# Normalizing the first block of rows ahead of the second's last statistics, in column parts, with a bias transposed by DMA and two loads merged

## The chip, the cores and the metric

The kernel runs on one core of a Trainium2 chip. The metric is the device time of one execution in microseconds (us), taken over several executions; lower is better. A difference counts as faster or slower from 2% (4.3 us) on. The span is the time from the first to the last instruction of a trace; the time of an execution is some 2 us longer. A few executions are in a slower state, in which the granted clock of TensorE is lower; unless said otherwise the compared runs are in the fast state.

## The reference, cut to what matters

```python
# B, S, D = 1, 2048, 640; H = 32 heads of 20; F = 1536; bf16
x  = A_x
xn = _layernorm(x, axis=-1)
return x + _A_ref(xn, A_wqkv, A_wo) + _B_ref(xn, B_w1, B_b1, B_w2, B_b2)
# _A_ref: q, k, v = xn @ wqkv; each position attends to 8 positions, 2 apart, then @ wo
# _B_ref: gelu(xn @ w1 + b1) @ w2 + b2
```

## The kernel before

The rows are handled in four chunks of 512, each of four blocks of 128. Every piece of work is a task with an engine, a rank, a duration, and an earliest time (`after`, used where a load has to land). A list scheduler at build time puts the tasks of TensorE (PE), VectorE (DVE), ScalarE (ACT) and the queue of SyncE (SP) in a fixed order. The engines then run in that order, whatever the real times are.

In chunk 0 each block goes through statistics, square root (ACT), reciprocal and normalization (DVE), five transposes (PE), and a copy out of PSUM (ACT). Then come its q, k and v projections, `gps`:

```python
# plan, chunk 0
land = (3.2, 3.2, 6.6, 6.6)[bl] if n == 0 else 11.4 + 1.9 * n
pl.add(f"st{n}{bl}", VE, 1.17, -40 if n else -99, [], f("st", n, bl), after=land)
pl.add(f"rs{n}{bl}", SE, 0.35, -99, [f"st{n}{bl}"], f("sqrt", n, bl, bl + 1), table="sqrt")
pl.add(f"rc{n}{bl}", VE, 0.17, -99, [f"rs{n}{bl}"], f("rstd", n, bl, bl + 1))
...
def do_tp(n, bl):                                  # five transposes into one PSUM tile
    xn = tiles["xn", n, bl]
    tp = psA.tile([P, 2 * CH], BF16, tag="acc", name="tp")
    for t in range(KT):
        nc.tensor.transpose(tp[:, t * P : (t + 1) * P], xn[:, t * P : (t + 1) * P], ident[:])
...
# loads, in the order in which SP issues them
nc.sync.dma_start(x_sb[:, 0, :], x_nb[:, 0, :])
for s in range(3):                                 # wq, wk, wv
    nc.sync.dma_start(wqkv[s][:], wqkv_v[:, :, s * D : (s + 1) * D])
    if s == 0:
        nc.sync.dma_start(x_sb[:, 2:BPC, :], x_nb[:, 2:BPC, :])
nc.sync.dma_start(b1_rt[0:FT, :], B_b1.rearrange("(t p) -> t p", p=P))
for n in range(1, NCH):                            # x of chunks 1, 2, 3
    ...
nc.sync.dma_start(w1_sb[:], B_w1.rearrange("(t p) n -> p t n", p=P))
...
def bias1():                                       # between k and v of block 0, on PE
    nc.tensor.transpose(b1_tp[:, 0:FT], b1_rt[0:FT, :], ident[0:FT, 0:FT])
    nc.vector.tensor_copy(b1T[:], b1_tp[:, 0:FT])
```

After chunk 0's projections come the first layer of the MLP (`hps`), the other chunks' projections (`pps`), the logits (`L`, which need the DVE's products `prod`), and the output (`lo`, `hi`).

## Time and profile before

| before | value |
|---|---|
| time, median of the first three executions | 215.12 us |
| time of the profiled execution | 215.21 us |
| PE busy | 206.1 us, 97% of a span of 212.9 us |
| first `gps` (first real dense matmul) | 7.70 us |
| first k projection; landing of wk | 9.93; 9.6 us |
| first `hps` | 25.32 us |
| last output piece on DVE | starts at 210.14 us |

The page's busy shares and chain, TensorE's list of waits and the head are shown with the prediction. One stretch is not shown there. It is the timeline of DVE around 10 to 14 us. The columns are start, duration, engine, line, operation, output and inputs, count, and in brackets the idle time before it and what ended that.

```profile
9.83 0.17 DVE L398 RECIPROCAL rstd<-std 128x1 f32<-128x1 f32 x1
9.91 0.27 DVE L363 TENSOR_REDUCE head_of<-ident 128x32 bf16<-128x128 bf16 x1
10.10 0.45 DVE L415 TENSOR_SCALAR xn<-x_sb,mv,rstd 128x640 bf16<-128x640 bf16 x1
12.47 0.17 DVE L370 CAST b1T<-b_tp 128x12 f32<-128x12 bf16 x1 [1.93 <-PE b_tp L369]
13.70 0.49 DVE L388 BATCH_NORM_STATS2 stats<-x_sb 128x6 f32<-128x320 bf16 x1 [1.05 <-DMA x_sb<-in_A_x_dram]
```

The `xn` at 10.10 is the last block of chunk 0. It is done 3 us before DVE turns to the statistics of chunk 1, for which it waits until x lands at 13.70.

The timeline of PE in the same kernel has the first k projection, b1's transpose, and the first `hps`:

```profile
9.93 1.28 PE L489 MATMUL gps<-xnT,wk_sb 128*128 128x128 bf16 x20
...
12.26 0.18 PE L369 MATMUL b_tp<-ident,b_rt 12*128 12x12 bf16 x1
...
25.32 1.03 PE L637 MATMUL hps<-xnT,w_sb 128*128 128x512 bf16 x3
```

### The profile page before, as it was taken

The numbers are of one execution on the slowest core, as the hardware profiler recorded it, in microseconds if no ns is written. First come the engines' busy times: TensorE is split into PE (matmuls) and PEld (weight loads), VectorE is DVE, ScalarE is ACT, GpSimd is POOL, SyncE is SP. The second block draws the span as 40 slices with busy tenths as digits, with TensorE's granted clock in tenths as the row PEclk, the third lists the DMA queues.
The fourth block names the chain that finished last, engine by engine and source line by source line (L and its number), as shares of the span: only waits on it lengthen the run. The fifth ranks groups of instructions, "written<-read, shape, count | busy, mean of one in ns | idle before, by whom it ended". The sixth has DMA issues, their size and how long they took to land.

```text
span 212.9 us, 3943 instructions
## 1 busy us (share of the span) xinstructions
PE 206.1 (97%) x1665; PEld 121.2 (57%) x1690; DVE 174.2 (82%) x176; ACT 106.8 (50%) x190; POOL 19.5 (9%) x36
## 2 busy tenths in 40 slices
PE   7899999999999999999999999999999999999994
PEld 7799844654544556556555555554555455555552
DVE  2849999459999999999999999999499789982001
ACT  3567899689565733635428273420297321351210
POOL 2000000000011015101001010110101011101220
PEclk9999999999999999999999999999999999999999
DMA  6999417973939579977002180211021822202223
GB/s 211 364 363 381 78 31 198 386 67 41 228 115 140 76 261 211 197 115 190 0 3 31 17 210 4 31 7 27 2 31 14 216 32 31 26 8 32 34 31 62
DMA packets 23433, 23.95 MB, mean 112 GB/s; under 512 B 9080, under 2 KB 20600, under 8 KB 23416
## 3 DMA queue, kind: packets, MB, share of 16 engines
q1 hardware_dynamic: 17832, 16.49, 28.0%
q0 software_dynamic: 4144, 4.92, 17.3%
q10 hardware_dynamic: 1440, 2.29, 3.7%
q8 instruction: 13, 0.21, 0.4%
q14 instruction: 4, 0.03, 0.0%
HBM read 10.00 MB, written 7.54 MB: 82 GB/s over the span
## 4 chain that ended last, share of the span: by engine, by line
PE 95%; DMA 1%; DVE 1%; issue 1%; ACT 0%
PE lo L668 26%; PE hps L637 24%; PE pps L472 23%; PE gps L489 8%; PE hi L670 8%; PE L L541 4%; DMA x_sb<-in_A_x_dram 1%; PE tp L429 0%; DVE stats L388 0%; DVE stats L389 0%; ACT xnT L433 0%; DVE xn L415 0%; DVE mv L390 0%; DVE osb L698 0%; PE b_tp L369 0%
## 5 line engine op out<-in xcount | busy, mean ns | idle before, releaser
L637 PE MATMUL hps<-xnT,w_sb 128*128 128x512 bf16 x236 | 53.9, 379 | 0.3 <-issue 0.2
L668 PE MATMUL lo<-w_sb,hT 128*128 128x512 bf16 x186 | 52.6, 379 | 0.0
L615 DVE TENSOR_TENSOR pv<-vT,ax 128x2560 bf16<-128x2560 bf16 x32 | 45.9, 1484 | 4.9 <-PE L L541 2.9
L522 DVE TENSOR_TENSOR prod<-qT,kT 128x2560 bf16<-128x2560 bf16 x32 | 45.5, 1484 | 0.0
L670 PE MATMUL hi<-w_sb,hT 128*128 128x128 bf16 x192 | 40.3, 219 | 0.3
L648 ACT ACTIVATE hT<-hps,b1T 128x512 bf16<-128x512 f32 x48 | 31.4, 687 | 17.0 <-PE hps L637 13.7
L637 PEld LDWEIGHTS <-w_sb 128*128 128x128 bf16 x240 | 22.8, 98 | 26.8 <-issue 0.4
L675 ACT CAST osb<-lo 128x512 bf16<-128x512 f32 x15 | 8.8, 585 | 50.9 <-PE hi L670 22.9
L624 DVE TENSOR_TENSOR pv<-pv 128x5120 bf16<-128x5120 bf16 x12 | 33.9, 2822 | 0.3
L668 PEld LDWEIGHTS <-hT 128*128 128x128 bf16 x192 | 18.7, 98 | 22.6 <-issue 0.2
L681 POOL DMA_DIRECT2D out_dram<-osb x15 | 12.9, 862 | 110.4 <-ACT osb L676 110.4
L668 PE MATMUL lo<-wo,oT 128*128 128x512 bf16 x74 | 22.1, 379 | 0.1
L670 PEld LDWEIGHTS <-hT 128*128 128x128 bf16 x192 | 18.4, 98 | 1.9
L670 PE MATMUL hi<-wo,oT 128*128 128x128 bf16 x80 | 16.9, 219 | 0.3
L472 PE MATMUL pps<-xnT,wk_sb 128*128 128x512 bf16 x71 | 16.9, 380 | 0.2
L472 PE MATMUL pps<-xnT,wq_sb 128*128 128x512 bf16 x72 | 16.9, 380 | 0.2
L472 PE MATMUL pps<-xnT,wv_sb 128*128 128x512 bf16 x73 | 16.9, 379 | 0.1
L689 DVE TENSOR_TENSOR osb<-lo,xlast 128x512 bf16<-128x512 f32 x1 | 0.7, 690 | 16.1 <-PE lo L668 16.1
L507 ACT CAST kT<-pps 128x512 bf16<-128x512 f32 x15 | 8.8, 584 | 8.8 <-PE pps L472 8.6
L668 PEld LDWEIGHTS <-oT 128*128 128x128 bf16 x80 | 7.8, 98 | 9.4
L472 PEld LDWEIGHTS <-wk_sb 128*128 128x128 bf16 x75 | 8.6, 118 | 7.5 <-issue 0.4
L472 PEld LDWEIGHTS <-wv_sb 128*128 128x128 bf16 x75 | 8.6, 117 | 7.2
(63 smaller groups left out, 208.2 us busy)
## 6 DMA issues: line engine op xcount, KB each, us to landing
w_sb<-in_B_w_dram SPq DMA_DIRECT2D x2, 1920.0 KB, 11.5
out_dram<-osb POOLq DMA_DIRECT2D x15, 160.0 KB, 3.4
ax<-attn SPq DMA_DIRECT2D x8, 256.0 KB, 5.1
ax<-attn ACTq DMA_DIRECT2D x8, 256.0 KB, 5.5
x_sb<-in_A_x_dram SPq DMA_DIRECT2D x3, 640.0 KB, 11.4
out_dram<-x_sb SPq DMA_DIRECT2D x3, 640.0 KB, 4.7
out_dram<-b2bc POOLq DMA_DIRECT2D x3, 640.0 KB, 7.7
wq_sb<-in_A_wqkv_dram SPq DMA_DIRECT2D x1, 800.0 KB, 4.9
```

Of the source, the lines that this page charges most:

```text
L472: nc.tensor.matmul(ps[:], lhsT=wqkv_p[which][:, ti, to, :], rhs=xnT[:, ti, :], start=(ti == 0), stop=(ti == KT - 1),)
L489: nc.tensor.matmul(ps[:, i, :], lhsT=wqkv_p[which][:, ti, to, :], rhs=tiles["xnT", 0][:, ti, cs], start=(ti == 0), stop=(ti == KT - 1),)
L507: nc.scalar.copy(dest[:, to, off : off + CH], tiles["pps", n, which, to][:])
L522: nc.vector.tensor_tensor(out=prod[:, i, :, :], in0=qkv_tile(n, 0)[:], in1=qkv_tile(n, 1)[:, :, off : off + CH], op=ALU.mult,)
L615: nc.vector.tensor_tensor(out=pv[:, i, :, :].rearrange("p t (j c) -> p t j c", j=BPC), in0=qkv_tile(n, 2)[:, :, off : off + CH].rearrange( ...
L624: nc.vector.tensor_tensor(out=ta[:], in0=ta[:], in1=tb[:], op=ALU.add)
L637: nc.tensor.matmul(ps[:], lhsT=w1_sb[:, ti, ft * P : (ft + 1) * P], rhs=tiles["xnT", n][:, ti, :], start=(ti == 0), stop=(ti == KT - 1),)
L648: nc.scalar.activation(hT[:], tiles["hps", n, ft][:], ACT.Gelu_apprx_tanh, bias=b1T[:, ft : ft + 1], scale=1.0)
L668: nc.tensor.matmul(lo[:], lhsT=lhs, rhs=rhs[:, 0:CH], start=first, stop=last)
L670: nc.tensor.matmul(hi[:, 0 : D - CH], lhsT=lhs, rhs=rhs[:, CH:D], start=first, stop=last)
L675: nc.scalar.copy(osb[:, 0:CH], tiles["lo", n, bl][:])
L681: nc.gpsimd.dma_start(rows, tiles["osb", n, bl][:], accum_op=ALU.add)
```

## The change

The intent is to start dense work earlier. The statistics of a block are split in halves, so that the first block's reciprocal goes ahead of the second block's last statistics. The first block's normalization, transposes, copies and first q projections go in two column parts. wk is loaded ahead of x of blocks 2 and 3. b1's transpose leaves PE for the DMA. Besides, x of the last two chunks is one load, the last residual is added in place, the warm-up uses a zeroed tile, and the ranks of many tasks are tuned anew. Cut to its core:

```diff
-WARM = 40
+WARM = 44
 RANK = { ... }                                    # 22 offsets replaced by 21 others
...
-            land = (3.2, 3.2, 6.6, 6.6)[bl] if n == 0 else 11.4 + 1.9 * n
-            pl.add(f"st{n}{bl}", VE, 1.17, -40 if n else -99, [], f("st", n, bl), after=land)
+            land = (4.0, 4.0, 9.6, 9.6)[bl] if n == 0 else (0.0, 13.3, 17.1, 17.1)[n]
+            r = -40 if n else -99
+            pl.add(f"st{n}{bl}a", VE, 0.5, r, [], f("st", n, bl, 0), after=land)
+            pl.add(f"st{n}{bl}", VE, 0.62, r, [f"st{n}{bl}a"] + ([f"rc{n}{bl - 1}"] if n == 0 and bl else []), ...)
...
+            for i, (a, b) in enumerate(((0, 2), (2, KT)) if bl == 0 else ((0, KT),)):
+                pl.add(f"xn{n}{bl}{u}", VE, 0.06 + 0.36 * us, -99, [f"rc{n}{bl}"], f("xn", n, bl, a, b), [xn])
+                pl.add(f"tp{n}{bl}{u}", PE, ..., [f"xn{n}{bl}{u}"], f("tp", n, bl, a, b), [xn, tp])
+                pl.add(f"tc{n}{bl}{u}", SE, 0.16 + 0.49 * us, -99, [f"tp{n}{bl}{u}"], f("tc", n, bl, a, b), [tp, xnT])
...
-        if s == 0:
+        if s == 1:
             nc.sync.dma_start(x_sb[:, 2:BPC, :], x_nb[:, 2:BPC, :])
-    for n in range(1, NCH):
-        cs = slice(n * BPC, (n + 1) * BPC)
+    for cs in (slice(BPC, 2 * BPC), slice(2 * BPC, NCH * BPC)):
         nc.sync.dma_start(x_sb[:, cs, :], x_nb[:, cs, :])
+    nc.sync.dma_start_transpose(b1_t[:], b1_rt[:])
...
-        tp = psA.tile([P, 2 * CH], BF16, tag="acc", name="tp")
+        tp = get(("tp", n, bl), lambda: psA.tile([P, 2 * CH], BF16, tag="acc", name="tp"))
-        for t in range(KT):
+        for t in range(a, b):
             nc.tensor.transpose(tp[:, t * P : (t + 1) * P], xn[:, t * P : (t + 1) * P], ident[:])
```

## The prediction

> **What bounds the kernel now.** I read the page first (part 1, busy time; part 4, the chain), then the waits of TensorE, then the timeline of the first 26 us engine by engine.
>
> ```profile
> PE 206.1 (97%) x1665; PEld 121.2 (57%) x1690; DVE 174.2 (82%) x176; ACT 106.8 (50%) x190; POOL 19.5 (9%) x36
> ...
> PE 95%; DMA 1%; DVE 1%; issue 1%; ACT 0%
> ```
>
> TensorE (PE) is busy 97% and is 95% of the chain that ended last. A busy PE need not be a PE without gaps, so the waits:
>
> ```profile
> PE idle L709 <- POOL ident masks.py:199: 1.5, 1, 1.5
> PE tp L429 <- DVE xn L415: 0.7, 1, 0.7
> PE gps L489 <- ACT xnT L433: 0.2, 1, 0.2
> PE hps L637 <- issue: 0.2, 1, 0.2
> ```
>
> These are all of PE's waits above the list's floor, and all but the last lie before 7.70 us, where the first real matmul of the projections starts. From there to the last matmul at 210.14 PE runs without a wait. The time is therefore (when dense work begins) + (sum of PE work) + a fixed tail of some 2.8 us. Only the first term and a few instructions of the second can be moved. The head, from the timeline:
>
> ```profile
> 3.78 0.49 DVE L388 BATCH_NORM_STATS2 stats<-x_sb 128x6 f32<-128x320 bf16 x1 [3.78 <-DMA x_sb<-in_A_x_dram]
> ...
> 4.95 0.29 ACT L394 ACTIVATE std<-mv,eps_t 128x1 f32<-128x1 f32 x1 [2.25 <-DVE mv L390]
> ...
> 5.82 0.11 DVE L398 RECIPROCAL rstd<-std 128x1 f32<-128x1 f32 x1
> ...
> 5.96 0.45 DVE L415 TENSOR_SCALAR xn<-x_sb,mv,rstd 128x640 bf16<-128x640 bf16 x1
> ...
> 6.47 1.00 PE L429 MATMUL tp<-ident,xn 128*128 128x128 bf16 x10 [0.72 <-DVE xn L415]
> 6.96 1.29 ACT L433 COPY xnT<-tp 128x640 bf16<-128x640 bf16 x2 [0.72 <-PE tp L429]
> ...
> 7.70 2.39 PE L489 MATMUL gps<-xnT,wq_sb 128*128 128x128 bf16 x40 [0.23 <-ACT xnT L433]
> ```
>
> The first block's standard deviation is ready at 5.24, but VectorE (DVE) takes its reciprocal only at 5.82, after all of the second block's statistics. That is the wait which the change attacks.
>
> **What the Trainium skill says.** (1) "TensorE: Matmul & The Clock Gate", section "Wait — 56ns, not 53.3ns?": start to start is 106.7 ns cold and 55.6 ns warm at 128 columns, 215.7 ns warm at 512. The trace agrees: 40 warm-up matmuls in 4.26 us are 106 ns each, 230 projections between 12.48 and 25.32 are 55.8 ns each, 45 hps between 25.32 and 35.03 are 215.8 ns each. I use these, not the 219 and 379 ns printed for one instruction. (2) Same page, "What's actually happening": warmth takes about 3.4 us of sustained activity. The warm-up still spans more than that. (3) "DMA: Bandwidth & Descriptors", "Queues, rings and completion order": on one DMA engine descriptors are consumed in ring order. So a load lands after what was issued before it, and moving one load ahead of another moves its landing. The trace agrees: wq, x of blocks 2 and 3, wk and wv, issued in that order, land at 6.1, 7.0, 9.6 and 11.8 us (issue plus time to landing: 1.20+4.9, 1.67+5.3, 2.23+7.4, 2.74+9.1). (4) "VectorE: DVE Perf Modes", "The three transpose paths": a 128x128 DMA transpose takes 1309 ns. This trace has only 128x640 ones, 3.2 us to landing; nothing here shows a small one behind large loads.
>
> **The change, part by part.**
>
> *Warm-up.* It now needs a DVE memset of zeros instead of GpSimd's identity, so it can start at some 0.9 us instead of 1.49. 44 x 106 ns = 4.7 us, ending near 5.6 instead of 5.75. It stays off the path.
>
> *First block ahead.* The order of DVE now has the first reciprocal right after half of the second block's statistics, which end at 5.27. With the hop of 0.09 us from ACT's end to a reciprocal (6.24 to 6.33 in the second block): reciprocal at 5.33, xn of the first two column tiles at 5.47 (0.14 later, as before). Splitting the measured 0.45 us by columns with 0.06 fixed, the two pieces end near 5.7 and 6.0. Transposes of the first piece follow 0.06 later, at 5.74. Before, five transposes to the copy took 0.49; two take 0.32. The copies (0.70 whole, split with 0.16 fixed: 0.38 and 0.48) run 6.06 to 6.44 and 6.44 to 6.92. The first eight q matmuls start at 6.48 and take 8 x 0.056 = 0.45, the other twelve start at 6.96 and end at 7.63. So the first matmul comes 7.70 - 6.48 = 1.2 us earlier.
>
> *What follows it.* In the new PE order come five transposes of block 1, then 20 k matmuls of block 0. The second block is now the later one: ACT's square root after the copies 6.92 to 7.22, reciprocal 7.31, xn 7.45 to 7.90, transposes 7.96 to 8.24. Then k needs wk. It now stands ahead of x of blocks 2 and 3, so 320 KB fewer lie before it: 1,920 KB instead of 2,240 with its own. The DMA throughput in the head adds up to 1,966,000 bytes at about 7.65 us; landings trail such sums by 0.7 us (wq) to 1.05 us (wk, wv), which gives 8.35 to 8.7. I take 8.6. Here PE waits 0.36 us, and the lead that block 0 won is mostly spent.
>
> *From wk on.* Left are 300 - 20 = 280 projection matmuls and 10 transposes: 280 x 0.0558 + 10 x 0.056 = 16.2 us, so hps would start at 24.8 instead of 25.32. **Gain: 0.5 us.** Contained in it is the removal of b1's transpose from PE: k ends near 12.17 and wv starts at 12.48 before, so 0.3 us goes there. The tightest later point is block 3: its xn now follows the statistics of block 4, whose x lands at 13.6. Counting on from 13.70 with 1.0 us of statistics, reciprocal, head_of and xn, its transposes are ready at 15.65; PE gets there at 15.86. It fits by 0.2 us.
>
> *b1 by DMA.* SyncE must wait for b1 to land (behind wv, about 12 us) before it issues the transpose, and only then w1, which before was issued at 8.81. But before, w1 took 14.3 us to landing (23.1), because it queued behind x. The x loads occupy the DMA engines to about 17 in both kernels, so an issue of w1 at 13 to 15 should still land near 23, before 24.8. DVE's conversion of b1 stands among statistics that reach it near 21.5. No cost on the path.
>
> *x of two chunks in one load; last block's residual in place; other ranks.* One issue fewer on SyncE and a tile fewer; neither is on the path. The new ranks reorder all four engines to the end, but the number of matmuls is the same, and they had no wait to remove. ACT gets two more table loads of 1.28 us, at 50% busy. The eighth prod of chunk 0 should end near 35.1, PE asks for it at about 36.6; the fourth transposed block of chunk 1 should land near 33.0 and is asked for at 33.4. Value: zero if nothing new waits.
>
> Sum: 215.12 - 0.5 = 214.6; as small trims of group switches are as likely as small new waits, I leave a tenth for a wk that lands a little sooner: **214.5 us**.
>
> **The rivals.** *(A) The whole lead survives.* For this wk must land before block 1's transposes end (8.24): then another 0.36 us, 214.2. Against it: the sum of bytes; for it: landings trail by less in the early head (0.7 for wq). *(B) w1 becomes the wait.* If the small transpose holds up the rings, or SyncE issues w1 so late that the queue runs dry after 17, every microsecond past 24.8 goes onto the time: landing at 26 makes 215.7. For it: nothing in the trace shows such a transpose in front of a load; against it: 2 to 4 us of other loads still queued when w1 is issued. *(C) The reordering brings a wait.* Candidates are the three tight points above, and later ACT with its added table loads holding PE's four accumulators. Each would cost 0.2 to 1 us: 214.8 to 215.5. Against it: the kernel before keeps PE fed for 200 us with the same rates, and DVE is busy 82%, ACT 50%. *(D) The head wins nothing*, because the wait only moves to wk and block 3's normalization: 215.1.
>
> **Range and chances.** My main course gives 214.5, A 214.2, C and D up to 215.3. More than 0.9 us of gain would need PE work to vanish, and there is none but b1's. Hence 213.9 to 215.3. 2% is 4.3 us; the head before the first matmul is only 7.7 us in all, and the load of x and its statistics (to 5.2) stay, so faster by 2% is all but excluded. Slower by 2% would need B at 29 us or several long new waits: 0.02.
>
> **What would show each step.** Right: first gps near 6.5; a PE wait of 0.2 to 0.5 us just before the first k matmuls, released by the load of wk; no b_tp; hps starting at 24.6 to 25.0; no PE wait after; the last matmul 0.5 us earlier. Wrong: first gps after 7 (split pieces cost more than their share); k at once after block 1's transposes (A); a wait before the first hps released by w1 (B); PE waits over 0.2 us on ACT or DVE after 25 us (C). Busy time of PE should fall by 0.3 us or stay. A last matmul earlier by more than 1 us would mean that I missed a gap in PE's stream.

## The result, and the profile after

| | before | changed |
|---|---|---|
| median of 6 executions each | 215.12 us | 214.97 us |
| lowest to highest | 214.94 to 215.41 | 214.41 to 215.42 |
| ratio changed/before, 95% interval | | 0.9989 (0.9971 to 1.0007) |
| first `gps` in the profile | 7.70 | 7.03 |
| first k projection | 9.93 | 8.64 |
| first `hps` | 25.32 | 24.86 |
| last output piece on DVE starts | 210.14 | 209.68 |

A ratio here is the mean time of one kernel's fast runs over that of the other's of the same rounds, so it is not quite the ratio of the medians quoted. The profiled execution of the changed kernel, 214.46 us, is one of its two fastest of six; that of the kernel before, 215.21 us, is slower than its median. This becomes important.

TensorE's list of waits in that execution (line, what was waited for, total us, times, longest):

```profile
PE idle L725 <- DVE zeros L361: 1.0, 1, 1.0
PE gps L501 <- ACT xnT L441: 0.5, 1, 0.5
PE hi L686 <- issue: 0.2, 1, 0.2
```

The wait for `xn` is gone; the wait for the copy `xnT` grew from 0.2 to 0.5 us. Nothing waits for wk or w1. The head in the timeline:

```profile
5.20 0.16 DVE L408 RECIPROCAL rstd<-std 128x1 f32<-128x1 f32 x1
5.40 0.63 DVE L424 TENSOR_SCALAR xn<-x_sb,mv,rstd 128x256 bf16<-128x256 bf16 x2
...
5.80 0.77 PE L437 MATMUL tp<-ident,xn 128*128 128x128 bf16 x5
...
6.61 0.75 ACT L441 COPY xnT<-tp 128x256 bf16<-128x256 bf16 x2 [1.44 <-PE tp L437]
7.03 1.28 PE L501 MATMUL gps<-xnT,wq_sb 128*128 128x128 bf16 x20 [0.46 <-ACT xnT L441]
...
8.29 0.45 PE L437 MATMUL tp<-ident,xn 128*128 128x128 bf16 x5
...
8.64 1.31 PE L501 MATMUL gps<-xnT,wk_sb 128*128 128x128 bf16 x20
...
13.58 0.89 DVE L398 BATCH_NORM_STATS2 stats<-x_sb 128x6 f32<-128x320 bf16 x2 [1.00 <-DMA x_sb<-in_A_x_dram]
...
14.85 0.45 DVE L424 TENSOR_SCALAR xn<-x_sb,mv,rstd 128x640 bf16<-128x640 bf16 x1
...
15.93 0.44 PE L437 MATMUL tp<-ident,xn 128*128 128x128 bf16 x5
```

The reciprocal comes at 5.20, as intended. The first copy comes only at 6.61, after all five transposes (5.80 to 6.57), though it needs two of them. k starts at 8.64, when both the transposes ahead of it are done and wk has landed (issued at 1.67, 6.9 us to landing: 8.57). And the last block of chunk 0 (`xn` at 14.85) now stands behind the load of chunk 1's x (13.58), where before it stood 3 us ahead of it.

**One landmark separates the head from the rest.** From the start of the first `hps` to the last output piece on DVE, the two profiles have 210.14 - 25.32 = 184.82 us before and 209.68 - 24.86 = 184.82 us after. Between these two points all the new ranks together are worth 0.00 us. Counting this way through all fourteen profiles, eleven have 184.81 or 184.82. The other three are e4_two_tp (185.35), e5_stats_after_xn3 (185.62) and e9_x_in_two_loads (185.01). So within the span, whatever the change does is done by the start of `hps`, and for the changed kernel and its variants the first `hps` says the time to 0.1 us in nine of twelve profiles: 24.86 + 189.6 = 214.46. In both profiles of the kernel before it is 189.9 (215.21 - 25.32 and 214.98 - 25.02).

**These 0.3 us lie outside the span.** Time and span:

| executions | median time | median span | time less span |
|---|---|---|---|
| call 1: before (11) | 215.38 | 213.1 | 2.23 to 2.56 |
| call 1: changed, e1 (6) | 215.36 | 213.25 | 2.07 to 2.16 |
| call 2: before (11) | 215.37 | 212.8 | 2.18 to 2.59 |
| call 2: changed, e8 (5) | 215.06 | 212.9 | 2.06 to 2.26 |

The mean of the last column is 2.4 us for the kernel before (2.4 in call 3 too) and 2.1 for the changed one (2.1 in the first comparison too). No step of the prediction and no trace shows what is shorter there. Of the variants only e2, with b1 back on PE, has values as in the kernel before, in four of its six executions (2.38 to 2.56; the other two 1.99 and 2.02). That is a hint at the b1 edit, and no more. Within the span, the median execution of the changed kernel is not shorter in either call (by the means it is 0.2 us shorter in call 1, where the spans scatter by 2 us, and equal in call 2).

That raises the question for the experiments. The head gained 0.46 us in this pair of profiles (and the pair's times differ by 0.75, with the 0.3 outside the span), but the medians differ by only 0.15 us. Where is the rest?

**My theory** going in: the head's gain is real, but the changed kernel runs closely behind loads, and in most executions some load lands later than in the profiled one. **Rival 1:** the gain is smaller because one part (the b1 transpose by DMA, the column parts, the merged load) costs something that another part wins. **Rival 2:** nothing was won, and the profiled execution was luck.

### The profile page after: what moved, and what is told of

Read it like the earlier page. It is cut to its first block, busy times and chain, and to the rows that moved or that the text cites. A ratio compares the mean times of both kernels' runs of the same rounds, so it can differ in the third digit from the quotient of the medians.

```text
span 212.4 us, 3961 instructions
## 1 busy us (share of the span) xinstructions
PE 206.9 (97%) x1670; PEld 121.7 (57%) x1693; DVE 174.4 (82%) x178; ACT 109.5 (52%) x193; POOL 19.7 (9%) x37
## 4 chain that ended last, share of the span: by engine, by line
PE 97%; issue 1%; DVE 0%; ACT 0%
PE lo L684 27%; PE hps L653 24%; PE pps L484 23%; PE gps L501 8%; PE hi L686 8%; PE L L557 4%; PE idle L725 2%; PE tp L437 1%; ACT xnT L441 0%; DVE osb L714 0%; DVE zeros L361 0%
## 5 line engine op out<-in xcount | busy, mean ns | idle before, releaser
L684 PE MATMUL lo<-w_sb,hT 128*128 128x512 bf16 x183 | 51.8, 379 | 0.0
L684 PE MATMUL lo<-wo,oT 128*128 128x512 bf16 x79 | 23.0, 379 | 0.0
L398 DVE BATCH_NORM_STATS2 stats<-x_sb 128x6 f32<-128x320 bf16 x32 | 14.0, 469 | 5.1 <-DMA x_sb<-in_A_x_dram 5.1
L705 DVE TENSOR_TENSOR osb<-lo,x_sb 128x512 bf16<-128x512 f32 x1 | 0.7, 692 | 16.1 <-PE lo L684 16.1
L520 ACT CAST qT<-pps 128x512 bf16<-128x512 f32 x15 | 8.8, 585 | 9.2 <-PE pps L484 9.2
```

The source lines that it names most:

```text
L398: nc.vector.bn_stats(stats[:, i, :], x_sb[:, b, i * (D // 2) : (i + 1) * (D // 2)])
L520: nc.scalar.copy(dest[:, to, off : off + CH], tiles["pps", n, which, to][:])
L684: nc.tensor.matmul(lo[:], lhsT=lhs, rhs=rhs[:, 0:CH], start=first, stop=last)
```

## The experiments

All kernels gave the right result. Runs of one call share a chip and 11 runs of the kernel before: call 1 (e1 to e4) 215.38 us median, call 2 (e5 to e8) 215.37, call 3 (e9 to e12) 215.22. In the diffs, `-` is the changed kernel.

### e1_again: the changed kernel unaltered

> The changed kernel unaltered. Accounting theory (the head's lead goes straight to the end): the 0.46 us by which its profiled run ended earlier is its usual gain, so ratio to before 0.998 and a median near 214.6. Rival (the lead is there only in some runs, and something that varies takes it back in others): ratio 0.999 or nearer 1, single times again spread over 1 us, and a profile that falls on a slow execution has a PE wait or a cold stretch that the first profile had not.

Measured: median 215.36 us (214.28 to 216.41), ratio 0.9979 (0.9939 to 1.0019). Its profile fell on its fastest execution, 214.28 us: k at 8.45, x of chunk 1 landed at 13.28, `hps` at 24.64, no wait but those in the profile above. So single executions reach the predicted time, but one execution is 1 us from the next, on the same chip.

### e8_after_third: the changed kernel unaltered, in the second call

> The changed kernel unaltered, as the base of this call. Ratio to before 0.997 to 0.999; spread about 1 us; if its profile falls on an execution of 215.2 or more, the theory of exposure expects a PE wait of 0.3 us or more before k (load of wk late) or before block 3's transposes (load of x late), and the rival expects neither.

Measured: median 215.06 us (214.96 to 215.15), ratio 0.9987 (0.9974 to 1.0000). This time the profile is of a usual execution, 215.07 us. Its list of PE waits has a new first line (0.33 of its 1.0 us lie before the first transposes):

```profile
PE tp L437 <- DVE xn L424: 1.0, 2, 0.7
```

The timelines of DVE and PE show where the 0.7 us are:

```profile
14.70 0.89 DVE L398 BATCH_NORM_STATS2 stats<-x_sb 128x6 f32<-128x320 bf16 x2 [2.45 <-DMA x_sb<-in_A_x_dram]
...
15.96 0.45 DVE L424 TENSOR_SCALAR xn<-x_sb,mv,rstd 128x640 bf16<-128x640 bf16 x1
...
16.46 0.45 PE L437 MATMUL tp<-ident,xn 128*128 128x128 bf16 x5 [0.70 <-DVE xn L424]
```

k started at 8.31 here, earlier than in the profile above. But x of chunk 1 landed at 14.70 instead of 13.58. DVE runs in its fixed order, so it sat idle for 2.45 us with the last block of chunk 0 to do. PE's previous 20 matmuls started at 14.48; without a wait the transposes follow 1.12 us later (14.81 to 15.93 in the profile above), at 15.60. They came at 16.46, so 0.86 us were lost, and `hps` started at 25.41. Had nothing waited, it would have been 25.41 - 0.86 = 24.55.

The margin is now measured. From the landing to the transposes is 16.46 - 14.70 = 1.76 us. In the profile above PE got there at 15.93, so a landing up to 14.17 was free there, and it was 13.58: a margin of 0.6 us. Across all profiles that load landed between 13.15 and 15.06 us. Counted in the same way, e4 lost 0.81 us at block 3 and e12 0.38.

### e5_stats_after_xn3: the same load, but not in front of block 3

```diff
+        at = next(i for i, t in enumerate(plan) if t["name"] == "xn03")
+        late = [t for t in plan[:at] if t["name"] in ("st10a", "st10")]
+        plan = [t for t in plan[: at + 1] if t not in late] + late + plan[at + 1 :]
```

> The changed kernel, with the statistics of block 4 (first of chunk 1) moved behind the normalization of block 3 on VectorE, nothing else. Theory of exposure (in the changed kernel block 3's transposes wait behind a VectorE instruction that waits for the load of x of chunk 1; this load has landed between 13.1 and 14.6 us in the profiles, and PE asks for the transposes near 15.9): no PE wait at block 3's transposes even if that load lands at 14.6, and the mean gains 0.1 to 0.3 us on the changed kernel of the same call with a narrower spread. Rival (the spread comes from wk's landing or the clock): same mean as the changed kernel within 0.1 us, same spread.

Measured, on the same chip as e8: median 214.85 us (214.27 to 216.41), ratio 0.9992 (0.9961 to 1.0023). In the profiled execution x of chunk 1 landed at 14.67, just as late as in e8. This is PE at the same place, and its one later wait:

```profile
15.91 0.44 PE L437 MATMUL tp<-ident,xn 128*128 128x128 bf16 x5
...
115.64 0.73 PE L557 MATMUL L<-prod,head_of 128*32 128x256 bf16 x20 [0.63 <-DVE prod L535]
```

The wait at block 3 is gone with the landing unchanged. From k to `hps` it took 24.85 - 8.65 = 16.20 us, against 25.41 - 8.31 = 17.10 in e8. That shows the mechanism: DVE's order, not the load alone, made PE wait. But the scatter did not narrow as I had expected. In this execution 0.63 us were lost again 90 us later, at the logits of chunk 2, which waited for a DVE product. e4 below has such a wait at the same place without this edit; e6, with it, has none. What brings it I did not find.

### e7_head_undone: both blocks' statistics first, block 0 in one piece

```diff
+        plan = [t for t in make_plan(fns).run() if t["name"] not in ("xn00a", "tp00a", "tc00a", "ga00")]
+        second = [t for t in plan if t["name"] in ("st01", "rs01")]
+        plan = [t for t in plan if t not in second]
+        at = next(i for i, t in enumerate(plan) if t["name"] == "rc00")
+        plan[at:at] = second
```

(With it xn00, tp00, tc00 and gj00 are run on all columns.)

> The changed kernel with its named head change undone: both blocks' statistics and the second's square root ahead of the first reciprocal, block 0 whole, as in the kernel before; loads, b1 by DMA and all later order stay as changed. Accounting theory: first q matmul back at 7.7, k at 9.1 (PE arrives after wk), hps near 25.3, time +0.45 us against the changed kernel. Rival (the head change is hidden behind wk's landing): k at 8.6 to 8.7, time as the changed kernel.

Measured: median 215.30 us (214.76 to 216.38, the two slowest at a granted clock of 0.992), ratio 1.0009 (0.9984 to 1.0034); e8, beside it, had 0.9987. The profile has the first `gps` at 7.50, `tp` of block 1 at 8.61 and k at 9.64, because wk landed only at 9.57. The direction agrees with the theory, 0.24 us between the medians, but the intervals overlap. I count it as consistent, not as decisive. What the order of the statistics does is seen at the first transpose: it comes 2.69 us after the first statistics here (6.27 and 3.58), as in the kernel before (6.47 and 3.78), and 2.09 us after them in the changed kernel (5.80 and 3.71).

### e12_no_columns: the order kept, the column parts undone

```diff
+        whole = {
+            "xn00": lambda: do_xn(0, 0), "tp00": lambda: do_tp(0, 0, 0, KT),
+            "tc00": lambda: do_tc(0, 0, 0, KT), "gj00": lambda: do_gj(0, 0, 0, KT),
+        }
         for t in make_plan(fns).run():
-            t["fn"]()
+            if t["name"] not in ("xn00a", "tp00a", "tc00a", "ga00"):
+                whole.get(t["name"], t["fn"])()
```

> The changed kernel with block 0 in one piece on all engines: only the column parts undone, the first reciprocal still ahead of the second block's last statistics. Since both pieces share one PSUM tile, the split gains only the shorter way from the second piece: first q matmul 0.1 us later than in the changed kernel (7.1), k at 8.6 to 8.7, time within 0.1 us of the changed kernel. Rival (the parts carry the gain): first q matmul 0.4 us later or more, time +0.3 us.

Measured: median 214.76 us (214.31 to 215.67), ratio 0.9976 (0.9955 to 0.9998). Its PE timeline:

```profile
7.40 1.28 PE L501 MATMUL gps<-xnT,wq_sb 128*128 128x128 bf16 x20 [0.78 <-ACT xnT L441]
8.52 0.44 PE L437 MATMUL tp<-ident,xn 128*128 128x128 bf16 x5
8.79 1.28 PE L501 MATMUL gps<-xnT,wk_sb 128*128 128x128 bf16 x20
```

The first `gps` is 0.37 us later than in the changed kernel's profile, where 0.1 was expected. By k 0.15 us of that are left, and counted from the first transpose 0.04 us (8.79 - 5.91 = 2.88 against 8.64 - 5.80 = 2.84). In time nothing was lost, though there was no changed kernel in this call to compare with. The column parts, as the changed kernel has them, are worth nothing that these runs can see. The lead at the first transpose is the order's: without the parts it is still 2.20 us after the first statistics (5.91 and 3.71).

### e4_two_tp: a PSUM tile for each column part

```diff
-        tp = get(("tp", n, bl), lambda: psA.tile([P, 2 * CH], BF16, tag="acc", name="tp"))
+        tp = get(("tp", n, bl, a), lambda: psA.tile([P, 2 * CH], BF16, tag="acc", name="tp"))
```

> The changed kernel with a PSUM tile of its own for each column piece of block 0's transposes. Theory of the shared tile (the first copy waited for all five transposes because both pieces write one tile): the first copy starts near 6.2 instead of 6.61, the first q matmul near 6.6 instead of 7.03, but k still starts at 8.6 because wk lands then; hps start and time unaltered within 0.2 us. Rival (the copy was late for another reason, such as the cold clock or the latency of PSUM): first copy at 6.6 as before.

Measured: median 215.05 us (214.29 to 215.65), ratio 0.9963 (0.9926 to 1.0000). The head of PE and ACT in the profile:

```profile
5.66 0.61 PE L437 MATMUL tp<-ident,xn 128*128 128x128 bf16 x5
6.12 0.75 ACT L441 COPY xnT<-tp 128x256 bf16<-128x256 bf16 x2 [1.19 <-PE tp L437]
6.54 1.28 PE L501 MATMUL gps<-xnT,wq_sb 128*128 128x128 bf16 x20 [0.27 <-ACT xnT L441]
```

e1, on the same chip with its transposes also at 5.66, had its first `gps` at 6.90, so the own tiles bring 0.36 us:

```profile
6.47 0.75 ACT L441 COPY xnT<-tp 128x256 bf16<-128x256 bf16 x2 [1.46 <-PE tp L437]
```

The first copy started 0.46 us after the first transpose (6.12), where e1 needed 0.81 (6.47). With the shared PSUM tile the copy waits for every transpose into the tile, also for those whose columns it does not read. The rival, a slow clock, has a part too, but the smaller one, as e6 shows. As time the 0.36 us could not be seen in this execution, because x of chunk 1 landed at 14.56 and PE waited 0.6 us at block 3; the medians of e4 and e1 differ by 0.31 us, within the scatter. The list puts that wait down to an ACT cast, but the late normalization stands right in front of it.

### e6_two_tp_stats_late: e4 and e5 together

> Both single edits together: a PSUM tile for each column piece, and block 4's statistics behind block 3's normalization. If both mechanisms hold: first q matmul near 6.6, k at the later of 8.2 and wk's landing, no wait at block 3's transposes, hps between 24.4 and 24.9, time 0.2 to 0.5 us under the changed kernel and about 0.8 under the kernel before: a version that beats both. If wk alone sets k's start: same hps start as the changed kernel, no gain.

The edit is both diffs. Measured: median 214.60 us (214.22 to 215.91), ratio 0.9980 (0.9954 to 1.0005). In the profile the first `gps` is at 6.48, and the wait that the prediction had placed in front of k appears. From the timelines of PE and ACT:

```profile
5.74 0.63 PE L437 MATMUL tp<-ident,xn 128*128 128x128 bf16 x5 [0.61 <-DVE xn L424]
...
6.06 0.82 ACT L441 COPY xnT<-tp 128x256 bf16<-128x256 bf16 x2 [0.96 <-PE tp L437]
...
6.48 1.29 PE L501 MATMUL gps<-xnT,wq_sb 128*128 128x128 bf16 x20
...
8.73 1.31 PE L501 MATMUL gps<-xnT,wk_sb 128*128 128x128 bf16 x20 [0.47 <-DMA wk_sb<-in_A_wqkv_dram]
```

So a still faster head only waits for wk. Here the first copy starts 0.32 us after the first transpose, as predicted for two transposes. e8, on the same chip, needed 0.67 with the shared tile (5.66 and 6.33), and the changed kernel's profile 0.81. The last 0.14 us are the clock: in that profile the warm-up took 4.87 us, slow to its end, and the five transposes behind it took 0.29 to 0.31 us each; in e8 the warm-up took 4.34 us and the transposes 0.22 to 0.23. The first transposes were slow in five of the twelve profiles of the changed kernel and its variants (in e4 in part), and in none of the two of the kernel before, which starts them later. x of chunk 1 landed at 15.06, the latest of all profiles, and cost nothing at block 3.

### e2_b1_on_pe: b1's transpose back on TensorE

```diff
-    nc.sync.dma_start_transpose(b1_t[:], b1_rt[:])
...
     def do_gj(bl, g, a, b):
+        if bl == 0 and g == 3:
+            bias1()
```

> The changed kernel with b1 transposed by TensorE again, order of all other instructions unaltered, no DMA transpose of b1. Accounting theory: one transpose and its switch go back into PE's dense stream: hps starts 0.25 to 0.3 us later than in the changed kernel (about 25.15), time +0.3 us. Rival (b1's place on PE is hidden, or the DMA transpose costs something itself by delaying w1's issue): hps starts at 24.9 or earlier, time as the changed kernel or less.

Measured: median 215.24 us (214.72 to 215.83), ratio 0.9981 (0.9944 to 1.0019), so no difference that the time could show. The profile shows one. PE between k and `hps`:

```profile
8.65 1.31 PE L500 MATMUL gps<-xnT,wk_sb 128*128 128x128 bf16 x20 [0.18 <-DMA wk_sb<-in_A_wqkv_dram]
...
12.97 0.18 PE L546 MATMUL b_tp<-ident,b_rt 12*128 12x12 bf16 x1
...
25.11 2.11 PE L657 MATMUL hps<-xnT,w_sb 128*128 128x512 bf16 x8
```

From k to `hps` are 25.11 - 8.65 = 16.46 us, against 24.86 - 8.64 = 16.22 in the changed kernel: b1 off PE is worth 0.24 us. No trace shows a cost elsewhere. In the changed kernel SP issues w1 at 13.27, in the kernel before at 8.81, and w1 is there before `hps` asks for it.

### e3_x_before_wk: x of blocks 2 and 3 ahead of wk again

```diff
-        if s == 1:
+        if s == 0:
             nc.sync.dma_start(x_sb[:, 2:BPC, :], x_nb[:, 2:BPC, :])
```

> The changed kernel with x of blocks 2 and 3 loaded ahead of wk, as before. Accounting theory (wk's landing binds PE after block 0): wk lands near 9.6 instead of 8.57, PE waits 1.0 us before the first k matmuls, hps starts near 25.9, time +1.0 us against the changed kernel. Rival (landing of wk is not what PE waits for; block 1's transposes and the copies are): k starts at 8.6 to 8.8 all the same, time within 0.3 us.

Measured: five fast executions with a median of 215.43 us (215.13 to 216.53) and one slow (219.25); ratio 0.9997 (0.9955 to 1.0039). The fast median is 0.07 us above e1's beside it, so the 1 us that was expected does not show in the time. PE's waits in its profile begin with

```profile
PE gps L501 <- DMA wk_sb<-in_A_wqkv_dram: 1.6, 1, 1.6
PE gps L501 <- DMA wq_sb<-in_A_wqkv_dram: 1.2, 1, 1.2
```

k started at 10.57. In this execution the landing of wk does bind PE. But the wait for wq is not the edit's: wq is issued ahead of both, and it also landed late in e7, e9 and e11. wk landed 3.1 us after wq here (10.5 and 7.4), 2.4 to 2.6 us after it in the profiles of the changed kernel and e1. So the swap of the two loads moves wk by some 0.6 us, and the rest of its lateness is wq's.

### e9_x_in_two_loads: the merged load undone

```diff
-    for cs in (slice(BPC, 2 * BPC), slice(2 * BPC, NCH * BPC)):
+    for cs in (slice(n * BPC, (n + 1) * BPC) for n in range(1, NCH)):
```

> The changed kernel with x of chunks 2 and 3 in two loads again, nothing else. Theory of the merged load (x of chunk 1 lands 1 us late, near 14.6 instead of 13.6, because the 1,280 KB load issued right behind it competes with it): x of chunk 1 lands at 13.3 to 13.7, no PE wait at block 3's transposes, time 0.3 to 0.7 us under the changed kernel, 214.4. Rival (the late landing belongs to the chip or the moment, not to the merging): landings scatter from 13.3 to 14.7 here too, time as the changed kernel, 214.9 to 215.1.

In the profiles up to then, x of chunk 1 had landed some 1.8 us after wv in the one profile of separate loads, and some 3.2 us after it in several of the merged one. So I suspected the merged load of delaying the load ahead of it. Measured: median 215.46 us (214.88 to 217.91), ratio 1.0021 (0.9984 to 1.0058). x of chunk 1 did land 1.8 us after wv, but wq and wk were late (PE waited 0.9 and 0.7 us), and the time did not fall. Over all profiles the distance is long in five of eleven with the merged load and in none of three without. That is a hint, and no more: the theory predicted a gain and there was none.

### e10_before_again: the kernel before, one look

> The kernel before, for a second profile of it on this chip. Under the theory of the merged load, x of chunk 1 lands at 13.5 to 13.8 as in its first profile. Under the rival it lands anywhere to 14.7, and in either case PE has no wait after 7.8 us, because here block 3's normalization stands ahead of the instruction that waits for that load.

Measured: 214.98 us; first `gps` at 7.40, wk landed at 9.03 and k started at 9.63, x of chunk 1 landed at 13.15, `hps` at 25.02. With two profiles of the kernel before, its margin at wk is 9.93 - 9.63 = 0.3 and 9.63 - 9.03 = 0.6 us; the changed kernel has 8.64 - 8.57 = 0.1. The kernel before had the earliest x of chunk 1 of all profiles and, with its normalization already done, could not use it.

### e11_candidate: a version for use

e6 with one more half of statistics, of the last chunk, moved behind chunk 0's products on DVE:

```diff
+        early = next(t for t in plan if t["name"] == "st30a")
+        plan.remove(early)
+        plan.insert(next(i for i, t in enumerate(plan) if t["name"] == "qk031") + 1, early)
```

> A candidate that should beat both: a PSUM tile for each column piece, block 4's statistics behind block 3's normalization, and the first half of block 12's statistics behind the eight products of chunk 0. If the waits seen at block 3's transposes (0.7) and at the logits (0.3 to 0.6) both come from VectorE's late start on x of chunk 1, neither is left, PE waits only for wk (0 to 0.5 us), hps between 24.4 and 24.9; median 214.2 to 214.4, 0.5 us or more under the changed kernel's 215.0. If the spread has other causes, median 214.6 or more.

Measured: median 214.45 us (214.03 to 215.72), ratio 0.9966 (0.9940 to 0.9992), the lowest median and the lowest single time (214.03). Its interval lies below 1 on the same chip as the kernel before, 215.22; it is still only a third of a percent, so "same" by the 2% rule. The changed kernel was not in that call, so against it only the ratios speak (0.9966 against 0.9979, 0.9987 and 0.9989), and the intervals overlap. The profile fell on an execution with late weights, 215.06 us:

```profile
PE gps L501 <- DMA wk_sb<-in_A_wqkv_dram: 0.7, 1, 0.7
PE gps L501 <- DMA wq_sb<-in_A_wqkv_dram: 0.6, 1, 0.6
```

In this execution it is the landing of the weights that limits the version. Its gain on the kernel before is also one within the span, 212.35 us against 212.8 in the median.

## Why the prediction was right or wrong

The time was in the range, and the class right. This says little: the range held the kernel before itself, and the gain in time contains 0.3 us outside the span that no term of the sum is about. That they made up for what the head gave back was luck. As an account of the profiled execution the mechanism of the sum was right; several of its terms were not.

- **Bound, landmark and value of the reordering: right.** `hps` at 24.86 against 24.8 predicted, and 184.82 us from there to the end in both kernels. Between these points the new ranks, the merged load and the residual in place bring nothing, and the two extra table loads cost nothing. PE's busy time, which was to fall or stay, rose from 206.1 to 206.9 us; 0.6 of it is the longer warm-up (4.87 against 4.26).
- **First matmul 1.2 us earlier, at 6.48: too early.** It was 7.03; "after 7" was the prediction's own sign of being wrong. The step that failed is the one from the transposes to the copy: "two take 0.32". The parts share a PSUM tile, so the copy waited for all five. It started at 6.61, not 6.06. Of these 0.55 us, 0.35 are the shared tile (0.67 in e8 against 0.32 in e6), 0.14 the slow clock, and 0.06 the first transpose (5.80 against 5.74). The prediction's second point, that warmth takes about 3.4 us and the warm-up spans more, did not hold in this execution: after 4.87 us of it the clock was still slow. With own tiles and a fast clock, in e6, the first `gps` is at 6.48. The copies' own durations were sized right: 0.373 and 0.484 us against 0.38 and 0.48. The normalization in parts was sized too low: "0.06 fixed" was measured as 0.345 us for 256 columns and 0.373 for 384, against 0.446 in one piece. From these three one can estimate 0.28 us fixed and 0.26 ns per column. This miss cost almost nothing, because the second piece starts before the first ends: they ended at 5.74 and 6.03, against 5.7 and 6.0.
- **k waits 0.36 us for wk at 8.6: right start, wrong reason in this profile, so luck.** wk landed at 8.57. But block 1's transposes were also ready only at 8.57 (8.29 and five times 0.056), not at 8.24, so PE arrived together with wk. They were late because ACT takes block 1's square root behind the late copies, at 7.25 instead of 6.92. The miss did not show in k's start because the later of two arrivals counts. Where the head was made faster (e6), the wait appeared, 0.47 us.
- **b1 off PE, 0.3 us: 0.24** (e2).
- **"It fits by 0.2 us" at block 3: the decisive term.** The tight point was named, and its margin in the profile was 0.6 us, more than I had allowed: the chain from the landing to the transposes takes 1.76 us, not 1.95, and the load landed 0.12 earlier. But I held it against one landing, 13.70 us, when the landing itself moves between 13.15 and 15.06. In e8 it cost 0.86 us, in e12 0.38; in both profiles of the kernel before it cost nothing. This is rival C, at one of the places where it was placed, and I counted it as a rival when it is part of the usual course.
- **Rival A** (all the lead survives) did not happen. Its sign, k at once after block 1's transposes, did: in e1 k starts at 8.45, when they are done (8.16 and five times 0.056), with wk there at 8.3. But they came late. **Rival B** (w1 binds) is excluded: no profile has a wait for w1. **Rival D** (the head wins nothing) holds for the column parts, by e12; for the head as a whole the difference of e7 is in favour of a gain but not decisive, and the median spans of e1 and e8 are on the rival's side.

Put together: from the first statistics on DVE to the first `hps` the kernel before takes 21.54 us in both of its profiles (25.32 - 3.78 and 25.02 - 3.48). The changed kernel takes 21.15 and 21.09 where x of chunk 1 landed early (24.86 - 3.71, and e1's 24.64 - 3.55), and 21.84 in e8, where it landed late (25.41 - 3.57). So the head wins 0.4 us when that load is early and loses 0.3 when it is late, because the changed kernel stands at block 3 behind a load that the kernel before did not need. The median spans of e1 and e8 show no gain left on the whole. The three ratios, 0.9989, 0.9979 and 0.9987, mean 0.2 to 0.5 us of gain in time, against 0.6 predicted; that is about the 0.3 us outside the span. e5 against e8 shows the give-back at block 3 in single executions with equal landings; its share in the median was not measured by itself.

Left open: what is 0.3 us shorter outside the span; why x of chunk 1 lands 1.8 us after wv in some executions and 3.2 us in others; why wq and wk are about 1 us late in some (e3, e7, e9, e11); why the clock rises sooner or later; and why the logits of chunk 2 waited in e4 and e5.

## What to carry to other kernels

When the head of a bound engine is made shorter, list for every later load how long it may land after its usual time before the engine waits, and set that beside how much its landing varies over several profiles, not beside one landing. Look also at what stands behind a wait in the fixed order of a helper engine: here DVE idled for a late load with finished input for another block at hand. And check in the trace whether work cut in parts runs as parts. Here the parts of the PSUM tile `tp` did not: its first reader waited for its last writer until each part had a tile of its own. The parts of `xn` and `xnT`, which also share a tile, did: the first transpose started at 5.80 and the second part of `xn` was written until 6.03. Last, compare spans as well as times, or a difference outside the trace is taken for one inside it.

## What the Trainium skill lacked or had wrong

- "TensorE: Matmul & The Clock Gate", section "Back-to-back issue gap", gives about 81 ns for 128 columns and 131 ns for 512 as sustained in a real kernel. Here streams with a weight load for each matmul ran at 55.8 ns (230 projections from 12.48 to 25.32) and 215.8 ns (45 `hps` from 25.32 to 35.03, one of them missing in the trace), which the page calls the isolated gap.
- "VectorE: DVE Perf Modes", section "The three transpose paths", gives 1309 ns for a 128x128 DMA transpose and 390 ns on TensorE. Behind other loads a 16x128 DMA transpose took 6.4 us to landing and 1.20 us of SP's issue, and on PE the b1 transpose cost 0.24 us; five warm transposes of 128x128 in a row took 0.28 us, start to next start (15.93 to 16.21 in the changed kernel), 0.056 us each; one alone lasts 0.22 us in the trace.
- "DMA: Bandwidth & Descriptors", section "Queues, rings and completion order", says that descriptors are consumed in ring order on one DMA engine, but not how much a landing varies from one execution to the next. The same load behind the same issues landed 13.28 and 14.70 us into two executions of one kernel.
